# A fused attention and mixer kernel on one core: the first batch's steps in another order, and group 2's q and k loaded in pairs of heads over 128 rows

## The chip, the cores and the metric

The kernel runs on one core of a Trainium2 chip. Its engines run side by side, each through its own instructions in their order: TensorE (PE, matmuls), VectorE (DVE), ScalarE (ACT), GpSimd (POOL) and SyncE (SP, which only issues transfers). An engine waits where an instruction needs what another engine or a transfer has not yet delivered. Transfers between the memory outside (HBM) and the on-chip buffers of 128 partitions ("rows" below) are issued by SP, ACT or POOL and carried out by 16 DMA engines. The metric is the time of one execution in microseconds on the device; lower is better.

## The reference

For q, k, v of shape (8 batches, 12 heads, 448 tokens, 64) in float32:

```
q_n = q / sqrt(mean(q*q) + 1e-6) * g_q          # and k_n with g_k
x   = softmax(q_n k_n^T / 8) v                  # heads side by side: (8, 448, 768)
u   = x + mix(x)                                # over the tokens, (448x32) then (32x448)
out = u + max(u @ w_ch1, 0) @ w_ch2             # 768 -> 3072 -> 768
```

So each batch has attention with normalised q and k, a low-rank mix along the tokens, and a two-layer network, whose matmuls are most of the work.

## The kernel before

A batch's 12 heads are handled as three **groups** of four heads, a group as two **pairs** of two heads. The groups are numbered through: 0 to 2 are batch 0, 3 to 5 batch 1, and so on; pairs 0 and 1 belong to group 0, 2 and 3 to group 1, 4 and 5 to group 2.

For each group SP loads q, k and v as float32 (`load_qk` L93, `load_v` L106) into three rotating sets of buffers qf, kf, vf. A row holds two heads' share: row p of half `a` (64 rows) holds 7 tokens of head `c` = 0 and 7 of head `c` = 1. For most groups the heads of one half are two apart (0 and 2, or 1 and 3), so one transfer over 128 rows does it (L100). Group 2 (`BESIDE`) has neighbouring heads in a half: heads 0 and 1 of the group in the first 64 rows, 2 and 3 in the last. It is loaded by two transfers of 64 rows for q and two for k.

Then, per group: squares of q and k (steps `sq`, L136), their sums (`sm`, DVE, L166), the inverse roots by a logarithm and an exponential on ACT (`rt`, L942 to L953), scaling to bfloat16 (`sc`, L955), transposes on PE (`turn`, L363) and the copies out of them with q's gain (`tq` L371) or without (`tk` L380). v is cast by POOL (`val`, L204), and behind `val` of group g SP gets the loads of group g + 3. For group 0 the squares, sums, roots and scalings are cut in two parts (`sqp`, `smp`, `rt0`, `scp`).

Per pair: `S` (L418) computes four blocks of scores into one of two PSUM buffers, `E` (L433) takes their exponentials on ACT, `V` (L490) multiplies with v in two halves, and `N` (L507) divides by the row sums. Two sets of exponentials are kept, so a pair's first `E` waits for the `V` of the pair two before.

Batch 0 then is mixed (`mt`, `mtc`, `mix`, `mc`, L644 to L666) with matrices made from U and V (`prepu`, `prepv` on POOL), and its network starts (`u`, L706, the first four blocks; from L693 on the ordinary loop). `w` issues one part of the weights' load from POOL's queue (L295, L303); `b.n` issues n small matmuls that only keep PE busy (L242); `ms` clears buffers for the mix and, before the change, the zeros in the second key buffer (L345 to L348).

The order of all these steps for batch 0 is written out by hand in the text `FRONT` (L897); `name:engine` says which engine does a step (a ScalarE, v VectorE, p GpSimd). The steps are issued in that order, and every engine goes through its own share of them in that order. From batch 1 on a planner with fixed costs interleaves attention with the network; it doesn't see `FRONT`.

Of the kernel before, what the change touches and what calls it, by code (L numbers as in the profile page):

```python
# [27 lines left out]
def kernel(  # L28
# [13 lines left out]
    nc = tc.nc  # L42
    B, H, S, D = q.shape
# [5 lines left out]
    NT = S // 64  # L49
    NJ = S // P  # L50
    SM = NJ * P
    R = S - SM
# [32 lines left out]
    staged, ssqs, normed = {}, {}, {}  # L85
# [7 lines left out]
    def load_qk(gi, i, eng=None):  # L93
        b, h0, n = groups[gi]
        if gi == BESIDE:
            for a in range(2):
                nc.sync.dma_start(staged[gi][i][a * R:(a + 1) * R].rearrange("p (c j) d -> p c (j d)", c=2),
                                  (q, k)[i][b, h0 + 2 * a:h0 + 2 * a + 2].rearrange("c (p j) d -> p c (j d)", j=NT))
            return
        src = (q, k)[i][b, h0:h0 + n].rearrange("(c a) (p j) d -> (a p) c (j d)", a=2, j=NT)  # L100
        (eng or nc.sync).dma_start(staged[gi][i].rearrange("p (c j) d -> p c (j d)", c=2), src)
# [26 lines left out]
    def load(gi):  # L128
        stage_tiles(gi)
        for i in range(2):  # L130
            load_qk(gi, i)
        load_v(gi)
# [94 lines left out]
    for i in range(2):  # L227
        load_qk(0, i)
# [3 lines left out]
    for i in range(2):  # L232
        load_qk(1, i)
# [19 lines left out]
    def fill_values(i, eng):  # L253
        va, vl = va_bufs[i], vl_bufs[i]
        eng.memset(va[:, :, D:D1], 1.0)
        eng.memset(vl, 0.0)
        for e in range(2):
            eng.memset(vl[e * R:(e + 1) * R, :, e * D1 + D:(e + 1) * D1], 1.0)

    def fill_keys(i, eng):  # L260
        eng.memset(kT_bufs[i][D:P, :, SM:S], 0.0)
        eng.memset(kT_bufs[i][0:D, :, S:], 0.0)

    for i in range(2):
        fill_values(i, nc.vector)
    fill_keys(0, nc.vector)
    for e in range(2):
        nc.gpsimd.tensor_mul(gp[:, e * D:(e + 1) * D], grow[:, 0, :], grow[:, 1, :])

    gg = consts.tile([P, 2], FP32)  # L270
# [74 lines left out]
    def fill_mixer():  # L345
        nc.gpsimd.memset(Uz, 0.0)
        fill_values(2, nc.gpsimd)
        fill_keys(1, nc.gpsimd)  # L348


    at = {"pe": 0.0, "act": 0.0, "dve": 0.0}
# [429 lines left out]
    for i, (b, pr) in enumerate(pairs):  # L781
        if b == 0:
            continue
        gi, a = divmod(i, 2)
# [77 lines left out]
    for n, (c, f, a) in enumerate(att):  # L862
        gi = a[0] if f is Rest else a[2] if f is Spair else None
# [6 lines left out]
    for b in range(B):  # L870
# [24 lines left out]
    mlp.extend((3.9 * w, down_end, (B - 1, cols[-1], piece), B - 1) for piece, w in enumerate((1.0, 0.67, 0.34)))  # L895

    FRONT = """  # L897
        sqp.0.1:a sqp.0.0:p gr smp.0.1 sqp.1.1:a sqp.1.0:p smp.0.0 rt0.0.1 smp.1.1 gains:p smp.1.0 rt0.1.1 pg rt0.0.0 b.22
        scp.0.1:v scp.1.1:p rt0.1.0 scp.0.0:v sq.1.0:a scp.1.0:p gg turn.0.0 sm.1.0 ms tq.0.0:a turn.0.1 b.17 w tk.0.0 rt.1.0
        sq.1.1:a tq.0.1:v S.0.1 sc.1.0:v S.0.0 b.13 sq.2.0:p E.0.0 sm.1.1 turn.1.0 E.0.1 S.0.2 val.0 tk.0.1 E.0.2 tq.1.0:v b.5  # L900
        sm.2.0 S.0.3 b.8 E.0.3 S.1.0 rt.1.1 tq.1.1:v sq.2.1:p S.1.1 V.0.1 E.1.0 sc.1.1:v b.7 E.1.1 S.1.2 turn.1.1 sm.2.1 E.1.2
        S.1.3 V.0.0 tk.1.0 val.1 E.1.3 N.0.1 rt.2 tk.1.1 sc.2.0:p sc.2.1:v S.2.0 V.1.0 E.2.0 S.2.1 prepu N.1.0 E.2.1 S.2.2
        N.0.0 V.1.1 w E.2.2 turn.2.1 N.1.1 prepv S.2.3 b.4 tk.2.0 E.2.3 S.3.0 E.3.0 tk.2.1 S.3.1 w turn.2.0 V.2.0 E.3.1 tq.2.1:v
        S.3.2 N.2.0 mt.0 E.3.2 tq.2.0:v S.3.3 V.2.1 val.2 mtc.0 E.3.3 S.4.0 N.2.1 E.4.0 S.4.1 V.3.1 w V.3.0 E.4.1 N.3.1 S.4.2
        mix.1 N.3.0 E.4.2 S.4.3 sq.3.0:p mt.1 mc.1:v E.4.3 S.5.0 mtc.1 E.5.0 S.5.1 V.4.0 sq.3.1:p V.4.1 E.5.1 N.4.0 S.5.2 mix.0
        N.4.1 E.5.2 S.5.3 mix.2 mc.0:v mix.3 E.5.3 sm.3.0 u.0.0 mc.2:a u.1.0 mt.2 mc.3:a u.0.1 u.1.1 mtc.2 V.5.0 sm.3.1 u.2.0
        u.2.1 V.5.1 N.5.0 rt.3 u.3.0 u.3.1 N.5.1 u.0.3 u.1.3 u.2.3 u.3.3 mt.3 u.0.2 mix.4 mtc.3 u.1.2 mix.5 mc.4:a u.2.2 u.3.2
        mc.5:a u.0.4 u.1.4 u.2.4 u.3.4 u.0.5 u.1.5 u.2.5 u.3.5
    """
    engines = {"a": nc.scalar, "v": nc.vector, "p": pool, "": None}  # L910
    beside = uT.rearrange("p k c -> p (k c)")[:, :4 * NT * D].bitcast(FP32).rearrange("p (j d) -> p j d", d=D)
# [43 lines left out]
    def scale_by(gi, i, eng, lo=0, hi=NT):  # L955
# [8 lines left out]
        "smp": lambda i, p, eng: sums_part(i, *PARTS[p]),  # L964
        "rt0": lambda i, p, eng: (log_part(i, p), root_part(i, p)),
        "ms": lambda eng: fill_mixer(),
        "scp": lambda i, p, eng: scale_by(0, i, eng, *PARTS[p]),
        "gr": lambda eng: most_gain(),
# [82 lines left out]
    while ia < len(att) or im < len(mlp):  # L1051
# [10 lines left out]
        if take_att:  # L1062
            c, f, a = att[ia]
# [13 lines left out]
        else:  # L1077
# [6 lines left out]
            c, f, a, _ = mlp[im]  # L1084
# [35 lines left out]
```

## Time and profile before

| | |
|---|---|
| timed runs, us | 3262.81, 573.63, 570.91; median 573.63 |
| profiled execution, us | 570.46 (its span 568.7) |
| PE busy | 561.5 us, 99% |
| ACT, POOL, DVE busy | 308.5, 204.5, 189.4 us |
| the first matmul of L693 | at 39.46 us |
| loads of q and k, 448 KB each | 23 and 23, landing in 3.7 and 4.9 us in the median |
| group 2's q and k, 224 KB each | 2 and 2, landing in 7.8 and 6.4 us in the median |

The profile shows one execution. Busy time is an engine's instructions added up; its share of the span says which engine is full. Where an engine is idle, the row of the next instruction tells how long and what ended the wait. The chain of waits follows the work that ended last back to the start, at each step to what released it. Columns of the windows' rows are: the stretch, its length, then the busy time and instruction count of PE, weight loads, DVE, ACT and POOL, PE's granted clock, the busy share of the DMA engines and what they moved in GB/s. In rows of transfers stand the count, the size of one, and the median time from issue to landing.

### The profile page before, as it was taken

The page shows a single profiled execution, that of the slowest core. Times are in us where ns is not written, and L with a number is a line of the kernel's source. Part 1 is how long each engine was busy: PE and PEld are TensorE (multiplying, and loading weights), DVE is VectorE, ACT ScalarE, POOL GpSimd, SP SyncE. Part 2 cuts the span into 40 slices and gives each one's busy share as a digit, 9 for nine tenths or more (in the row PEclk, how much of TensorE's full clock was granted, in tenths as well). Part 3 has the DMA queues.
Part 4 walks back from the last instruction along what each step waited for, and adds up shares of the span by engine and source line. Part 5 has one row for each costly group of instructions (what it writes and reads, how often), then busy time and mean ns, then how long its engine had stood idle before and what let it go on. Part 6 is the DMA issues. An engine that isn't in the chain of part 4 may idle for free.

```text
span 568.7 us, 11567 instructions
## 1 busy us (share of the span) xinstructions
PE 561.5 (99%) x4756; PEld 321.9 (57%) x4756; DVE 189.4 (33%) x425; ACT 308.5 (54%) x518; POOL 204.5 (36%) x308
## 2 busy tenths in 40 slices
PE   8899999999999999999999999999999999999997
PEld 7665555555555555555556555565465555555555
DVE  6955564312443222521235231532034210410011
ACT  6967760888454776287553677367752544014300
POOL 6874784355332724343522532351531000000000
PEclk9999999999999999999999999999999999999999
DMA  9999999784247633595335735375215200320022
GB/s 241 223 242 240 247 228 179 159 225 114 62 91 171 170 98 63 90 233 144 74 96 107 203 90 125 67 204 128 36 33 86 56 23 0 77 56 0 1 57 56
DMA packets 104830, 68.20 MB, mean 120 GB/s; under 512 B 66633, under 2 KB 100937, under 8 KB 104777
## 3 DMA queue, kind: packets, MB, share of 16 engines
q1 hardware_dynamic: 95124, 57.83, 44.2%
q0 software_dynamic: 9408, 9.44, 10.0%
q8 instruction: 37, 0.61, 0.5%
q10 hardware_dynamic: 244, 0.20, 0.1%
q14 instruction: 17, 0.13, 0.1%
HBM read 52.20 MB, written 11.01 MB: 111 GB/s over the span
## 4 chain that ended last, share of the span: by engine, by line
PE 94%; ACT 4%; DMA 1%; DVE 0%; POOL 0%; issue 0%; POOLq 0%
PE po L740 38%; PE ph L693 37%; PE pv L541 4%; ACT E L435 3%; PE sc L464 2%; PE sl L455 2%; PE sl L476 2%; PE pr L568 1%; PE po L727 1%; PE pv L537 1%; PE sc L430 1%; PE sc L711 1%; PE sc L626 1%; PE pu L609 1%; DMA ob<-in_g_k_dram 1%; PE pt L368 1%
## 5 line engine op out<-in xcount | busy, mean ns | idle before, releaser
L693 PE MATMUL ph<-uT,w1b 128*128 128x448 bf16 x1128 | 223.9, 352 | 0.0
L740 PE MATMUL po<-w2b,hT 128*128 128x384 bf16 x1296 | 223.5, 326 | 0.0
L740 PEld LDWEIGHTS <-hT 128*128 128x128 bf16 x1296 | 122.8, 98 | 84.1 <-issue 7.0
L693 PEld LDWEIGHTS <-w1b 128*128 128x128 bf16 x1128 | 108.2, 98 | 97.6 <-issue 2.2
L700 ACT ACTIVATE hT<-ph 128x448 bf16<-128x448 f32 x187 | 99.7, 550 | 106.9 <-PE ph L693 106.5
L399 POOL TENSOR_SCALAR qT<-qT,gg 128x448 bf16<-128x448 bf16 x36 | 50.4, 1402 | 92.4 <-DMA qT<-qn 77.3
L457 ACT ACTIVATE E<-sl,gg 128x448 bf16<-128x448 f32 x72 | 41.6, 630 | 76.2 <-PE sl L455 75.3
L198 POOL TENSOR_TENSOR qn<-qf,rs 128x384 bf16<-128x384 f32 x36 | 29.9, 830 | 111.9 <-ACT rs L175 106.1
L468 ACT ACTIVATE E<-sc,gg 128x896 bf16<-128x896 f32 x72 | 68.9, 1019 | 0.0
L750 DVE TENSOR_TENSOR ob<-po,x 128x384 f32<-128x384 f32 x46 | 25.6, 557 | 103.7 <-PE po L740 103.0
L167 DVE TENSOR_REDUCE ssq<-sq 128x14 f32<-128x896 f32 x45 | 47.0, 1078 | 23.9 <-ACT sq L141 23.2
L545 DVE RECIPROCAL r<-pv 128x6 f32<-128x6 f32 x42 | 8.2, 195 | 125.4 <-PE pv L541 125.1
L435 ACT ACTIVATE E<-sc,gg 128x896 bf16<-128x896 f32 (+1 forms) x42 | 37.0, 951 | 1.1 <-PE sc L430 0.7
L541 PE MATMUL pv<-va,E 128*128 128x65 bf16 x756 | 35.4, 194 | 0.0
L541 PEld LDWEIGHTS <-E 128*128 128x128 bf16 x756 | 32.4, 98 | 3.2
L198 POOL TENSOR_TENSOR kp<-kf,rs 128x384 bf16<-128x384 f32 x36 | 29.8, 828 | 0.0
L537 PE MATMUL pv<-vl,E 128*128 128x130 bf16 x126 | 27.6, 219 | 0.0
L633 DVE TENSOR_TENSOR x<-sc,x 128x384 bf16<-128x384 f32 x42 | 20.8, 550 | 17.4 <-PE sc L626 17.4
L546 DVE TENSOR_TENSOR x<-pv,r 128x384 bf16<-128x384 f32 x42 | 23.4, 557 | 1.4
L174 ACT ACTIVATE rs<-ssq,eps 128x28 f32<-128x28 f32 x20 | 6.3, 315 | 32.1 <-DVE ssq L167 32.1
L477 ACT ACTIVATE E<-sl,gg 128x448 bf16<-128x448 f32 x36 | 23.3, 646 | 0.0
L206 POOL CAST va<-vf 128x768 bf16<-128x768 f32 x24 | 20.7, 862 | 0.2 <-DMA vf<-in_v_dram 0.2
(130 smaller groups left out, 426.4 us busy)
## 6 DMA issues: line engine op xcount, KB each, us to landing
qf<-in_q_dram SPq DMA_DIRECT2D x23, 448.0 KB, 3.7
kf<-in_k_dram SPq DMA_DIRECT2D x23, 448.0 KB, 4.9
vf<-in_v_dram SPq DMA_DIRECT2D x48, 192.0 KB, 5.5
out_dram<-ob SPq DMA_DIRECT2D x48, 192.0 KB, 2.7
w2b<-in_moe_w_ch_dram POOLq DMA_DIRECT2D x8, 576.0 KB, 15.3
w1b<-in_moe_w_ch_dram POOLq DMA_DIRECT2D x2, 1152.0 KB, 17.6
vf<-in_v_dram SPq DMA_DIRECT2D x48, 32.0 KB, 5.1
w1b<-in_moe_w_ch_dram POOLq DMA_DIRECT2D x1, 1536.0 KB, 28.5
```

Source lines behind the costliest of these rows:

```text
L167: nc.vector.tensor_reduce(ssqs[gi][:, i, :], sqs.pop((gi, i)), AX, ALU.add)
L198: nc.gpsimd.tensor_tensor(main.rearrange("p (t i) d -> p i t d", i=2), src[:, c, :2 * NJ].rearrange("p (i t) d -> p i t d", i=2), rs[:, c, ...
L399: nc.gpsimd.tensor_scalar(qT[:, a], qT[:, a], gg[:, 0:1], None, ALU.mult)
L435: nc.scalar.activation(es[(b, pr)][:, 2 * r:2 * r + n, :], sc[:, :n, :S], AF.Exp, scale=scal, bias=bias)
L457: nc.scalar.activation(E[:, 4 + i, :], ts[i], AF.Exp, scale=scal, bias=bias)
L468: nc.scalar.activation(E[:, 2 * r:2 * r + 2, :], tiles[r][:, :, :S], AF.Exp, scale=scal, bias=bias)
L537: nc.tensor.matmul(pv[:, i].rearrange("p e d -> p (e d)"), E[:, 2 * NJ, w:w + P], vl[:, lp, :], start=True, stop=False)
L541: nc.tensor.matmul(pv[:, i, e, :], E[:, 2 * j + e, w:w + P], va[:, (lp + 2 * e) * NJ + j, :], start=False, stop=(e == 1 and j == NJ - 1))
L693: nc.tensor.matmul(ph, w1b[:, dt, ht * P:(ht + 1) * P], uT[:, dt, off:off + S], start=(dt == 0), stop=(dt == KD - 1))
L700: nc.scalar.activation(hT[:, ht, off:off + S], ph, AF.Relu)
L740: nc.tensor.matmul(po, hT[:, ht, col:col + P], w2b[:, ht, half * HALF:(half + 1) * HALF], start=(ht == 0), stop=(ht == KH - 1))
L750: nc.vector.tensor_tensor(ob[:, h], po, urows(b, col, half), ALU.add)
```

## The change

Three edits.

1. Group 2's q and k are still loaded by two transfers each. Each now fills one of the two head slots (`c`) of all 128 rows, from two heads that are two apart, instead of both slots of 64 rows from two neighbouring heads. What lies where in the buffers afterwards is the same.
2. The zeros in the second key buffer are written by DVE at the start, with those of the first, instead of by POOL in `ms`.
3. `FRONT` has another order, other engines for some steps (sq.1.0 on POOL instead of ACT; sqp.1.0 and sqp.1.1 change places between ACT and POOL; scp.0.1 on POOL and scp.1.1 on DVE instead of the other way round; sc.1.0 on POOL instead of DVE) and other counts of the small matmuls (120 in all instead of 76).

```diff
         if gi == BESIDE:
-            for a in range(2):
-                nc.sync.dma_start(staged[gi][i][a * R:(a + 1) * R].rearrange("p (c j) d -> p c (j d)", c=2),
-                                  (q, k)[i][b, h0 + 2 * a:h0 + 2 * a + 2].rearrange("c (p j) d -> p c (j d)", j=NT))
+            for c in range(2):
+                nc.sync.dma_start(staged[gi][i][:, c * NT:(c + 1) * NT].rearrange("p j d -> p (j d)"),
+                                  (q, k)[i][b, h0 + c:h0 + c + 3:2].rearrange("a (p j) d -> a p (j d)", j=NT))
             return
...
-    fill_keys(0, nc.vector)
+    for i in range(2):
+        fill_keys(i, nc.vector)
...
         fill_values(2, nc.gpsimd)
-        fill_keys(1, nc.gpsimd)
...
     FRONT = """
-        sqp.0.1:a sqp.0.0:p gr smp.0.1 sqp.1.1:a sqp.1.0:p smp.0.0 rt0.0.1 smp.1.1 gains:p smp.1.0 rt0.1.1 pg rt0.0.0 b.22
-        scp.0.1:v scp.1.1:p rt0.1.0 scp.0.0:v sq.1.0:a scp.1.0:p gg turn.0.0 sm.1.0 ms tq.0.0:a turn.0.1 b.17 w tk.0.0 rt.1.0
-        sq.1.1:a tq.0.1:v S.0.1 sc.1.0:v S.0.0 b.13 sq.2.0:p E.0.0 sm.1.1 turn.1.0 E.0.1 S.0.2 val.0 tk.0.1 E.0.2 tq.1.0:v b.5
-        sm.2.0 S.0.3 b.8 E.0.3 S.1.0 rt.1.1 tq.1.1:v sq.2.1:p S.1.1 V.0.1 E.1.0 sc.1.1:v b.7 E.1.1 S.1.2 turn.1.1 sm.2.1 E.1.2
-        S.1.3 V.0.0 tk.1.0 val.1 E.1.3 N.0.1 rt.2 tk.1.1 sc.2.0:p sc.2.1:v S.2.0 V.1.0 E.2.0 S.2.1 prepu N.1.0 E.2.1 S.2.2
-        N.0.0 V.1.1 w E.2.2 turn.2.1 N.1.1 prepv S.2.3 b.4 tk.2.0 E.2.3 S.3.0 E.3.0 tk.2.1 S.3.1 w turn.2.0 V.2.0 E.3.1 tq.2.1:v
-        S.3.2 N.2.0 mt.0 E.3.2 tq.2.0:v S.3.3 V.2.1 val.2 mtc.0 E.3.3 S.4.0 N.2.1 E.4.0 S.4.1 V.3.1 w V.3.0 E.4.1 N.3.1 S.4.2
-        mix.1 N.3.0 E.4.2 S.4.3 sq.3.0:p mt.1 mc.1:v E.4.3 S.5.0 mtc.1 E.5.0 S.5.1 V.4.0 sq.3.1:p V.4.1 E.5.1 N.4.0 S.5.2 mix.0
-        N.4.1 E.5.2 S.5.3 mix.2 mc.0:v mix.3 E.5.3 sm.3.0 u.0.0 mc.2:a u.1.0 mt.2 mc.3:a u.0.1 u.1.1 mtc.2 V.5.0 sm.3.1 u.2.0
...
+        sqp.0.1:a sqp.0.0:p gr smp.0.1 gains:p sqp.1.0:a smp.0.0 sqp.1.1:p pg b.26 rt0.0.1 smp.1.0 rt0.0.0 scp.0.1:p smp.1.1
+        rt0.1.0 scp.0.0:v rt0.1.1 scp.1.0:p scp.1.1:v turn.0.0 sq.1.0:p gg turn.0.1 tq.0.0:a b.14 tk.0.0 sq.1.1:a S.0.0 w sm.1.0
+        S.0.1 b.17 E.0.0 sm.1.1 sq.2.0:p rt.1.0 S.0.2 b.18 E.0.1 tk.0.1 E.0.2 tq.0.1:v S.0.3 val.0 b.8 sm.2.0 rt.1.1 S.1.0 b.10
+        E.0.3 sc.1.1:v sc.1.0:p E.1.0 S.1.1 V.0.1 E.1.1 turn.1.1 S.1.2 sq.2.1:p tk.1.0 turn.1.0 E.1.2 S.1.3 V.0.0 tq.1.0:v E.1.3
+        tq.1.1:v S.2.0 N.0.1 E.2.0 val.1 S.2.1 b.11 sm.2.1 E.2.1 S.2.2 V.1.0 N.0.0 rt.2 tk.1.1 w V.1.1 E.2.2 S.2.3 sc.2.1:v b.9
+        w E.2.3 S.3.0 N.1.1 turn.2.1 E.3.0 sc.2.0:p N.1.0 S.3.1 V.2.1 E.3.1 tk.2.0 S.3.2 b.7 tk.2.1 E.3.2 ms turn.2.0 S.3.3
+        prepu V.2.0 tq.2.0:v E.3.3 tq.2.1:v S.4.0 prepv N.2.0 mt.0 E.4.0 S.4.1 mtc.0 V.3.0 val.2 E.4.1 S.4.2 N.3.0 V.3.1 E.4.2
+        N.2.1 w S.4.3 mix.0 N.3.1 E.4.3 mix.1 S.5.0 mc.0:v S.5.1 E.5.0 V.4.1 mc.1:v sq.3.0:p mt.1 N.4.1 E.5.1 S.5.2 V.4.0 mtc.1
+        E.5.2 sm.3.0 mix.3 sq.3.1:p mix.2 S.5.3 u.0.0 N.4.0 E.5.3 u.1.0 u.0.1 u.1.1 mc.2:a mt.2 sm.3.1 u.2.0 V.5.0 V.5.1 mtc.2
...
     """
```

More of the change, by code (lines that the diff above doesn't have):

```diff
@@ L906 @@
-        N.4.1 E.5.2 S.5.3 mix.2 mc.0:v mix.3 E.5.3 sm.3.0 u.0.0 mc.2:a u.1.0 mt.2 mc.3:a u.0.1 u.1.1 mtc.2 V.5.0 sm.3.1 u.2.0
-        u.2.1 V.5.1 N.5.0 rt.3 u.3.0 u.3.1 N.5.1 u.0.3 u.1.3 u.2.3 u.3.3 mt.3 u.0.2 mix.4 mtc.3 u.1.2 mix.5 mc.4:a u.2.2 u.3.2
-        mc.5:a u.0.4 u.1.4 u.2.4 u.3.4 u.0.5 u.1.5 u.2.5 u.3.5
+        sqp.0.1:a sqp.0.0:p gr smp.0.1 gains:p sqp.1.0:a smp.0.0 sqp.1.1:p pg b.26 rt0.0.1 smp.1.0 rt0.0.0 scp.0.1:p smp.1.1
+        rt0.1.0 scp.0.0:v rt0.1.1 scp.1.0:p scp.1.1:v turn.0.0 sq.1.0:p gg turn.0.1 tq.0.0:a b.14 tk.0.0 sq.1.1:a S.0.0 w sm.1.0
@@ new lines @@
+        prepu V.2.0 tq.2.0:v E.3.3 tq.2.1:v S.4.0 prepv N.2.0 mt.0 E.4.0 S.4.1 mtc.0 V.3.0 val.2 E.4.1 S.4.2 N.3.0 V.3.1 E.4.2
+        N.2.1 w S.4.3 mix.0 N.3.1 E.4.3 mix.1 S.5.0 mc.0:v S.5.1 E.5.0 V.4.1 mc.1:v sq.3.0:p mt.1 N.4.1 E.5.1 S.5.2 V.4.0 mtc.1
+        E.5.2 sm.3.0 mix.3 sq.3.1:p mix.2 S.5.3 u.0.0 N.4.0 E.5.3 u.1.0 u.0.1 u.1.1 mc.2:a mt.2 sm.3.1 u.2.0 V.5.0 V.5.1 mtc.2
+        rt.3 N.5.0 mix.4 mc.3:a u.2.1 N.5.1 u.3.0 mc.4:a u.3.1 u.0.3 u.1.3 mt.3 u.2.3 u.3.3 mtc.3 u.0.2 u.1.2 u.2.2 mix.5 u.3.2
@@ L909 @@
+        u.0.4 mc.5:a u.1.4 u.2.4 u.3.4 u.0.5 u.1.5 u.2.5 u.3.5
     """
```

## The prediction

> **What bounds the kernel now.** The page first: whether one engine fills the span, and at which clock.
>
> ```profile
> span 568.7 us, 11567 instructions
> PE 561.5 (99%) x4756; PEld 321.9 (57%) x4756; DVE 189.4 (33%) x425; ACT 308.5 (54%) x518; POOL 204.5 (36%) x308
> PEclk9999999999999999999999999999999999999999
> ```
>
> PE is busy for 99% of the span at full clock, and nothing in the change touches the multilayer part that fills it. So the question is when PE reaches that part, the first matmul of L693. The timeline of PE gives the place, the timeline of ACT what comes before it.
>
> ```profile
> 7.99 1.40 PE L245 MATMUL busy<-ident 128*128 128x128 bf16 x22
> ...
> 39.46 1.30 PE L693 MATMUL ph<-uT,w1b 128*128 128x448 bf16 x6
> ...
> 8.63 0.93 ACT L141 ACTIVATE sq<-qf 128x896 f32<-128x896 f32 x1
> ...
> 10.71 0.31 ACT L944 ACTIVATE rs<-ssq,eps 128x14 f32<-128x14 f32 x1
> ...
> 12.01 3.31 ACT L435 ACTIVATE E<-sc,gg 128x896 bf16<-128x896 f32 x4
> ...
> 18.85 0.33 ACT L944 ACTIVATE rs<-ssq,eps 128x28 f32<-128x28 f32 x1
> ...
> 19.43 13.55 ACT L435 ACTIVATE E<-sc,gg 128x896 bf16<-128x896 f32 x16
> 32.88 0.96 ACT L664 CAST uT<-ph 128x448 bf16<-128x448 f32 x2
> ```
>
> The front, the first batch's attention, takes 39.46 us. From 12.01 to 32.88 ACT goes from exponential to exponential almost without a gap; then 39.46 - 32.88 = 6.6 us of PE work end it. The chain of waits agrees: it runs over ACT there.
>
> ```profile
> 12.10 3.22 ACT E L435 x4
> ...
> 15.73 3.24 ACT E L435 x4
> ...
> 20.52 5.71 ACT E L435 x7
> ...
> 26.27 3.34 ACT E L435 x4
> ```
>
> The loads hide behind this only because they land early. The profiled execution took 570.46 us, 1.8 beyond its span; the three timed runs have a median of 573.63 with 570.91 as their lowest, so I work from 570.46. About 2%, here 11.4 us, is what a measurement of this kernel can tell from no change.
>
> **The change, the loads.** Group 2's q and k are now two transfers each of 224 KB as before, by 128 rows instead of 64. These rows show the present ones, their time to land, and the rates of all engines together (last column, GB/s; the share before it is of 16 engines).
>
> ```profile
> 2.78 1.42 SPq L97 DMA_DIRECT2D qf<-in_q_dram  x2
> ...
> 7.22 3.17 SPq L97 DMA_DIRECT2D kf<-in_k_dram  x2
> ...
> w1b<-in_moe_w_ch_dram POOLq DMA_DIRECT2D x1, 768.0 KB, 9.9
> ...
> qf<-in_q_dram SPq DMA_DIRECT2D x2, 224.0 KB, 7.8
> kf<-in_k_dram SPq DMA_DIRECT2D x2, 224.0 KB, 6.4
> ...
> ob<-in_moe_V_dram SPq DMA_DIRECT2D x1, 224.0 KB
> ...
> 2.00:3.00 1.00, 1.00 (x12) 1.00 (x11) 0.15 (x2) 0.01 (x1) 0.00 (x0) 1.00 0.91 224
> 3.00:4.00 1.00, 1.00 (x13) 1.00 (x10) 0.00 (x0) 0.00 (x0) 0.00 (x0) 1.00 1.00 353
> 4.00:5.00 1.00, 1.00 (x15) 1.00 (x14) 0.23 (x2) 0.52 (x1) 0.57 (x3) 1.00 1.11 378
> 5.00:6.00 1.00, 1.00 (x22) 1.00 (x20) 0.46 (x1) 0.45 (x2) 1.00 (x3) 1.00 0.96 344
> 6.00:7.00 1.00, 1.00 (x20) 0.91 (x17) 0.87 (x2) 0.45 (x3) 1.00 (x2) 1.00 1.03 364
> ...
> 13.00:14.00 1.00, 1.00 (x15) 0.65 (x12) 1.00 (x3) 1.00 (x2) 1.00 (x2) 1.00 1.10 237
> ```
>
> While 128-row loads run (3 to 7 us) all engines move 344 to 378 GB/s; later, with 64-row loads in flight, they are as busy and move 237. So 128 rows, dealt over all engines, would be the better form: 229 kB in 0.6 us.
>
> But the source of the new transfer has a pair of heads as its outermost dimension: the heads are two apart, so head and row don't merge into one dimension of 128, as they do in the loads of the other groups (L100), and the row isn't outermost, as it is in the present form (L98). If a transfer is dealt over the engines along its outermost dimension, the old form has 64 to deal and the new one 2: two engines carry it. One engine moves 378/16 = 23.6 GB/s, so 229 kB take 4.85 us on two engines, and the four transfers, if they share the same two, 19.4 us instead of the 2.4 that they would take on all. These are the two ends of the unknown price. No row settles it: moe_V's load, whose outermost dimension is 4 (L321), has a row without a time to land. I take two engines, because the code gives the dimension and the rows show nothing that could deal out a dimension of 2 to 16 engines.
>
> The Trainium skill, "DMA: Bandwidth & Descriptors", section "Why a DMA increments its semaphore by 16 and not by 1", states this: each access pattern's slowest dimension is looked at, and the largest count up to 16 that divides both sides is used, on the lowest-numbered engines. By it the new form runs on 2 engines, always the same two; no view of this profile shows the count.
>
> **The sum, along these two engines.** The four loads of groups 0 and 1 come first, 4 x 459 kB = 1.84 MB. The rows add up to 1.66 MB at 7.0 us, so they are through at 7.5. Group 2's q: two transfers, 9.7 us, to 17.2. Behind it in the queue stands each engine's share of group 0's v, 459/16 = 28.7 kB, at 237/16 = 14.8 GB/s 1.9 us; and the first weights, 768 KB issued by POOL, take their turns on the same engines, 49 kB each, 3.3 us: 22.4. Group 2's k: 9.7 us, 32.1; landed and seen, an estimate, at 33.
>
> What waits for it is in the rows of POOL and DVE (this square is group 2's k):
>
> ```profile
> 13.96 0.84 POOL L206 CAST va<-vf 128x768 bf16<-128x768 f32 x1
> ...
> 15.46 1.68 POOL L144 TENSOR_TENSOR sq<-kf 128x896 f32<-128x896 f32 x1
> 17.32 0.83 POOL L206 CAST va<-vf 128x768 bf16<-128x768 f32 x1 [0.18 <-DMA vf<-in_v_dram]
> ...
> 17.18 1.08 DVE L167 TENSOR_REDUCE ssq<-sq 128x14 f32<-128x896 f32 x1
> ...
> 22.55 0.90 POOL L295 DMA_DIRECT2D w1b<-in_moe_w_ch_dram  x1
> ```
>
> The square starts at 15.46 now and at 33 then. On POOL val.1, two weight issues and sc.2.0 are queued behind it (sc.2.0 from 33 + 1.7 + 1.5 + 1.8 = 38; it feeds the fifth pair's exponentials, due at about 41); on DVE N.0.0, tk.1.1 and sc.2.1 behind its sum; on ACT rt.2 waits for the sum, with E.2.2 and all later exponentials behind it. From 33: square 1.68, sum 1.08, rt.2 0.58 (18.85 to 19.43): 36.3. The row of sixteen exponentials lasts from 19.43 to 32.88, 13.45 us; in the new order two of them (E.2.0, E.2.1, 0.9 each) stand ahead of rt.2, so 13.45 - 1.8 = 11.65 are left: 48.0. Then the 6.6 us of the end: 54.6. L693 starts 54.6 - 39.5 = 15.1 us later, and since PE has no slack after it, the sum is 570.46 + 15.1 = **585.5 us**. V.0.1 slips too (val.0 waits for v, through at 22.4), but to about 24, well before 33.
>
> Loads behind these slip as well: v of groups 1 and 2, U and V are issued in order on SP behind them, and group 3's behind val.0. They land by about 40 to 50, when their users have slipped by the same 15. I take nothing for that and keep 3 us for the range.
>
> **The other edits.** The order by itself: sq.1.0 (0.93) leaves ACT for POOL and a part of the first squares comes back; rt.1.0 (0.31 and a second step) moves behind the first exponential. ACT gains at most 0.93 + 0.31, say 1 us, before its first exponential. ms moves on POOL from ahead of sq.2.0 to behind sc.2.0; the first weight issue stays ahead of sq.2.0, with sq.1.0 in front of it where ms was. The fillers grow from 76 to 120, 44 at 1.40/22 = 0.064, 2.8 us of PE; PE isn't the bound in the front, so they cost nothing as long as ACT is, and at most 2.8 if not. sm.3.0 now stands ahead of N.4.0 on DVE: if group 3's q lands late, N.4.0, mt.2 and the rest wait for it, up to 2 us by the row of group 2's k (6.4 to land). So the order alone lies between -1 and +3. Behind the late landing it is hidden; what it gives there is the two exponentials, already in the sum.
>
> ```profile
> 10.84 0.20 POOL L261 MEMSET kT<- 64x128 bf16 x1
> 11.10 0.20 POOL L262 MEMSET kT<- 64x128 bf16 x1
> ...
> 1.89 0.11 DVE L261 MEMSET kT<- 64x64 uint32 x1
> ...
> 4.77 0.21 DVE L276 TENSOR_REDUCE ob<-ob 1x1 f32<-1x64 f32 x1 [2.57 <-POOL ob L268]
> ```
>
> The zeros of the second key buffer leave POOL (two of 0.20) for DVE. DVE idles 2.57 us there, which hides them; without that cover they would cost about 0.2, two of 0.11.
>
> **Rivals.** *All engines.* The new loads are dealt over 16 engines. For it: 128 rows are what the fast loads have, 378 against 237 GB/s. Then k lands before 15.46 and the front stays ACT's: -1 for the order, **569.5**, no change or a little faster. It decides if k(2) lands before about 17. The Trainium skill, "DMA: Bandwidth & Descriptors", section "Rules for kernel authors", bids to replace two transfers to halves of the partitions by one of 128; by that rule alone this rival would hold, and the rates above agree with it for whole loads.
> *Two engines, but nothing queued behind.* If v and the weights pass the slow transfers instead of taking turns with them, 5.2 us go: k lands at 27.8, the end is 9.9 later, **580.5**.
> *Two engines and a longer trail.* Group 3 to 5's loads slip by more than PE does, or the two engines move less than 23.6 GB/s beside other traffic (14.8 as in the last rate row would give 7.8 us a transfer, 12 us more): 589.5 to 597, around **591**.
>
> **How the numbers follow.** Forecast 0.62, with a range of its own of 581.5 to 589 (k landing 4 us earlier or later); all engines 0.13; nothing queued 0.12; longer trail 0.13. The range 578 to 592 leaves out the first rival and 0.06 at the ends. Slower by over 2% (above 581.9): nearly all of the forecast and the long trail, 0.71; within 2%: 0.28; faster by over 2%: 0.01, since the front offers no 11 us that these edits could take.
>
> **What would show it.** In the changed kernel's DMA share a hollow between about 9 and 30 us, with few GB/s; POOL's square of group 2's kf (L144) waiting for its load until about 33, for some microseconds; ACT idle before rt.2; the first L693 at about 54. If kf is squared at 15 to 17 and no hollow shows, the step "two engines" is wrong. If the front is 15 us longer but the time isn't, PE has slack that I didn't see.

## The result, and the profile after

| | before | after |
|---|---|---|
| median of the timed runs, us | 571.83 (6 runs) | 590.94 (6 runs) |
| lowest and highest, us | 570.62 to 573.63, and a first run of 3262.81 | 589.51 to 593.5 |
| profiled execution, us | 570.46 | 593.22 |
| the first matmul of L693, us | 39.46 | 62.22 |
| profiled execution less that, us | 531.00 | 531.00 |

The change makes the kernel slower: the ratio is 1.0344, with an interval of 1.031 to 1.0378, or 19.1 us between the medians. The profile shows one execution, and it is one of the two longest of the six (593.2 and 593.5; the other four took 589.5 to 591.0). Its 22.8 us more lie entirely ahead of the first matmul of L693; the last row of the table says that nothing is gained or lost behind it.

The page of the changed kernel, the lines that answer to those of before and the DMA row of its 40 slices (14.8 us each):

```profile
span 591.4 us, 11655 instructions
PE 568.5 (96%) x4800; PEld 327.3 (55%) x4800; DVE 188.8 (32%) x426; ACT 308.9 (52%) x517; POOL 207.5 (35%) x308
PEclk9678999999999999999999999999999999999999
DMA  6469999978444763349452762268313410130022
```

PE has fallen from 99% to 96% of the span, and the second to fourth slices, up to 59 us, show a PE clock of 0.6 to 0.8, which the page of before doesn't. In the second and third the DMA engines are half idle although the kernel waits for loads. By stretches of 5 us (the last three columns are PE's granted clock, the busy share of the 16 DMA engines, and GB/s):

```profile
15.00:20.00 5.00, 0.66 (x9) 0.38 (x7) 0.00 (x0) 2.04 (x3) 0.00 (x0) 0.82 0.64 118
20.00:25.00 5.00, 0.00 (x0) 0.00 (x0) 2.08 (x2) 0.00 (x0) 2.90 (x4) 0.50 0.14 38
...
30.00:35.00 5.00, 1.40 (x24) 1.02 (x22) 0.00 (x0) 1.41 (x2) 1.35 (x1) 1.00 0.18 49
```

From 20 to 25 us the share is 0.14, and 0.14 of 16 is 2.2 engines (2.0 if measured against 1.12, the share from 45 to 50 us, when all are busy). In the trace a median of two packets are under way at a time in this stretch, and of 18 from 45 to 50 us. The two engines move 38 GB/s, 19 for each. That is a mean: loads of v and the weights take turns with q and k there. Where group 2's q or k moves alone, two engines move 50 to 52 GB/s, about 25 each:

```profile
8.00:9.00 1.00, 1.00 (x22) 1.00 (x20) 0.69 (x2) 0.35 (x2) 1.00 (x2) 1.00 0.13 52
...
24.00:25.00 1.00, 0.00 (x0) 0.00 (x0) 0.28 (x1) 0.00 (x0) 0.94 (x3) 0.50 0.13 50
```

Of the six such stretches of before, from 5 to 35 us, the following has the lowest share:

```profile
20.00:25.00 5.00, 4.60 (x67) 3.16 (x64) 4.76 (x18) 4.90 (x7) 4.88 (x8) 1.00 0.91 217
```

Who waits in this hollow is in the rows of POOL, DVE and ACT (start, duration; in brackets the idle time ahead and what ended it):

```profile
20.50 1.67 POOL L144 TENSOR_TENSOR uT<-qf 128x896 f32<-128x896 f32 x1 [8.80 <-DMA qf<-in_q_dram]
23.71 0.82 POOL L206 CAST va<-vf 128x768 bf16<-128x768 f32 x1 [1.55 <-DMA vf<-in_v_dram]
33.65 1.68 POOL L144 TENSOR_TENSOR sq<-kf 128x896 f32<-128x896 f32 x1 [6.75 <-DMA kf<-in_k_dram]
...
35.36 1.09 DVE L167 TENSOR_REDUCE ssq<-sq 128x14 f32<-128x896 f32 x1 [5.66 <-POOL sq L144]
...
36.48 0.32 ACT L944 ACTIVATE rs<-ssq,eps 128x28 f32<-128x28 f32 x1 [5.07 <-DVE ssq L167]
...
37.05 0.99 ACT L435 ACTIVATE E<-sc,gg 128x896 bf16<-128x896 f32 x1
38.49 0.63 ACT L435 ACTIVATE E<-sc,gg 128x448 bf16<-128x448 f32 x1 [0.45 <-PE sc L430]
39.94 1.01 ACT L435 ACTIVATE E<-sc,gg 128x896 bf16<-128x896 f32 x1 [0.82 <-PE sc L430]
...
51.16 0.63 ACT L435 ACTIVATE E<-sc,gg 128x448 bf16<-128x448 f32 x1 [0.29 <-PE sc L430]
```

Group 2's k is squared at 33.65 instead of 15.46; the sum, the root and every exponential from E.2.2 on stand behind it. The chain of waits ends the front with a second late load:

```profile
24.73 10.46 DMA vf<-in_v_dram
...
35.22 0.63 SPq L111
...
38.56 14.43 DMA kf<-in_k_dram
...
53.12 1.69 POOL sq L144
...
54.84 1.09 DVE ssq L167
55.92 0.21 DVE x L652
56.13 0.05 issue
56.18 0.56 PE ph L657
```

This is group 3's k. Its sum stands on DVE ahead of the copy (L652) that PE's mix needs. It was issued at 38.56, although val.0, behind which its load is placed, was over at 25.1. SP issues in order, and ahead of this load it had the rest of U, V and group 2's v: one load of U waited 3.4 us for group 2's k, and group 2's v (L111 at 35.22) for the v load issued at 24.73.

That it then took 14.4 us to land fits two weight loads of 1152 KB which POOL issued just ahead of it, from 36.67. The new order does the same with the old loads, and e8 and e9 below, which differ in the place of these two issues alone, show the price: group 3's k is squared at 36.69 in e8, after a wait for its load, and at 31.70 in e9, where the weights are issued behind it (and it is issued 1.3 us earlier), without a wait.

### The profile page after: what moved, and what is told of

Read it like the earlier page. It is cut to its first block, busy times and chain, and to the rows that moved or that the text cites. A ratio compares the mean times of both kernels' runs of the same rounds, so it can differ in the third digit from the quotient of the medians.

```text
span 591.4 us, 11655 instructions
## 1 busy us (share of the span) xinstructions
PE 568.5 (96%) x4800; PEld 327.3 (55%) x4800; DVE 188.8 (32%) x426; ACT 308.9 (52%) x517; POOL 207.5 (35%) x308
## 4 chain that ended last, share of the span: by engine, by line
PE 90%; DMA 5%; SPq 4%; ACT 0%; POOL 0%; DVE 0%; issue 0%; POOLq 0%
PE po L740 36%; PE ph L693 36%; PE pv L541 4%; DMA kf<-in_k_dram 2%; PE sc L464 2%; SPq L111 2%; PE sl L455 2%; DMA vf<-in_v_dram 2%; PE sl L476 2%; PE pr L568 1%; PE po L727 1%; PE pv L537 1%; SPq L97 1%; SPq L116 1%; PE sc L711 1%; PE sc L626 1%
## 5 line engine op out<-in xcount | busy, mean ns | idle before, releaser
L693 PE MATMUL ph<-uT,w1b 128*128 128x448 bf16 x1128 | 223.9, 352 | 0.0
L693 PEld LDWEIGHTS <-w1b 128*128 128x128 bf16 x1128 | 108.1, 98 | 97.7 <-issue 2.2
L167 DVE TENSOR_REDUCE ssq<-sq 128x14 f32<-128x896 f32 x45 | 47.0, 1079 | 32.9 <-ACT sq L141 23.2
```

What stands on the lines that cost most here:

```text
L167: nc.vector.tensor_reduce(ssqs[gi][:, i, :], sqs.pop((gi, i)), AX, ALU.add)
L693: nc.tensor.matmul(ph, w1b[:, dt, ht * P:(ht + 1) * P], uT[:, dt, off:off + S], start=(dt == 0), stop=(dt == KD - 1))
```

## The experiments

All of these compute the whole reference. Ratios are against the kernel before on the same chip, whose medians in the three groups of runs were 572.91, 571.86 and 571.35 us.

**e1, the order without the loads.** The changed kernel with the old loads:

```diff
-            for c in range(2):
-                nc.sync.dma_start(staged[gi][i][:, c * NT:(c + 1) * NT].rearrange("p j d -> p (j d)"),
-                                  (q, k)[i][b, h0 + c:h0 + c + 3:2].rearrange("a (p j) d -> a p (j d)", j=NT))
+            for a in range(2):
+                nc.sync.dma_start(staged[gi][i][a * R:(a + 1) * R].rearrange("p (c j) d -> p c (j d)", c=2),
+                                  (q, k)[i][b, h0 + 2 * a:h0 + 2 * a + 2].rearrange("c (p j) d -> p c (j d)", j=NT))
```

> The changed kernel with group 2's q and k loaded as before (64 rows at a time, the row outermost). Theory, two engines: the loss goes with the load, so 568 to 573 us, group 2's k squared at 15 to 18 us and L693 starting at 38 to 42. Rival, the order is what costs: about 588 to 592 us, L693 at 58 to 62 us, with the load landing early.

Measured: 577.45 us, ratio 1.0078 (1.0048 to 1.0109). The hollow and the long waits are gone, so the loads are the main part; but 4.5 us are left, more than the 3 that I had allowed the order. DVE's and PE's rows say where:

```profile
36.42 1.09 DVE L167 TENSOR_REDUCE ssq<-sq 128x14 f32<-128x896 f32 x1 [2.53 <-POOL sq L144]
37.42 0.17 DVE L513 RECIPROCAL r<-pv 128x4 f32<-128x4 f32 x1
37.63 0.42 DVE L514 TENSOR_TENSOR x<-pv,r 128x256 bf16<-128x256 f32 x1
39.82 1.09 DVE L167 TENSOR_REDUCE ssq<-sq 128x14 f32<-128x896 f32 x1 [1.76 <-POOL sq L144]
40.82 0.28 DVE L652 CAST x<-pu 128x128 bf16<-128x128 f32 x1
```

```profile
PE pu L648 <- DVE x L514: 2.1, 1, 2.1
PE ph L657 <- DVE x L652: 1.5, 1, 1.5
```

The sums of group 3's squares (L167) stand ahead of the division (L514) and of the copy (L652), wait 2.5 and 1.8 us for squares of data that has just landed, and PE waits behind them. The last exponential ends at 35.85 there, L693 starts at 47.04: an end of 11.2 us, with old loads.

**e2, the loads without the order.** The kernel before with the new form of the loads, the reverse of the diff above.

> The kernel before, with only the new load of group 2's q and k. Theory, two engines: k lands at about 33 us as in the changed kernel; all sixteen exponentials stand behind it here instead of fourteen, so at least as slow as the changed kernel, 589 to 595 us. Rival, the order is what costs: about 571 us.

Measured: 591.42 us, ratio 1.0323 (1.0283 to 1.0362), as much as the whole change. k is squared at 35.57:

```profile
35.57 1.68 POOL L144 TENSOR_TENSOR sq<-kf 128x896 f32<-128x896 f32 x1 [8.41 <-DMA kf<-in_k_dram]
```

The loads alone make the loss; that the order adds to it, or takes from it, doesn't show in the time. The rows do differ:

```profile
44.60 10.09 ACT L435 ACTIVATE E<-sc,gg 128x896 bf16<-128x896 f32 x12 [0.29 <-PE sc L430]
...
61.17 1.30 PE L693 MATMUL ph<-uT,w1b 128*128 128x448 bf16 x6
```

The last exponential ends at 54.69, 2.9 us later than in the changed kernel, and the end takes 6.5 us instead of 10.4. In the order of before the sums of group 3's squares start at 54.19 and 55.43 and hold nothing up, although its loads are as late (issued at 39.41 and 39.98).

**e3, the same bytes dealt by rows.** Each new transfer is cut into two of one head and 64 rows, so that the rows are the outermost dimension; the pieces that go to one row are as long as before.

```diff
-            for c in range(2):
-                nc.sync.dma_start(staged[gi][i][:, c * NT:(c + 1) * NT].rearrange("p j d -> p (j d)"),
-                                  (q, k)[i][b, h0 + c:h0 + c + 3:2].rearrange("a (p j) d -> a p (j d)", j=NT))
+            for a in range(2):
+                for c in range(2):
+                    nc.sync.dma_start(staged[gi][i][a * R:(a + 1) * R, c * NT:(c + 1) * NT].rearrange("p j d -> p (j d)"),
+                                      (q, k)[i][b, h0 + 2 * a + c].rearrange("(p j) d -> p (j d)", j=NT))
```

> The changed kernel with each of the four new transfers cut in two, one head and 64 rows each: the same head slots, the same 1792 bytes to a row, twice as many transfers, but the outermost dimension of the source is 64 and not 2. Theory, dealt along the outermost dimension: 568 to 574 us, k squared before 20 us. Rival, filling one head slot at a time in pairs of heads is what costs, whatever the engines: 588 to 592 us. A third, more transfers in the queue cost by themselves: between the two, about 575.

Measured: 579.21 us, ratio 1.0112 (1.0068 to 1.0156), about what e1 took: the order's cost, which I hadn't expected when I wrote 568 to 574, and little else. k is squared at 20.27, and its wait is no longer for the load:

```profile
20.27 1.68 POOL L145 TENSOR_TENSOR sq<-kf 128x896 f32<-128x896 f32 x1 [2.57 <-DVE x L515]
```

Bytes and the length of the pieces are those of the changed kernel, so these don't explain the loss. What differs is the outermost dimension, and that there are twice as many transfers of half the size. The number isn't it either: e1 has as many transfers as the changed kernel, with the 64 rows outermost, and its k doesn't wait.

**e4, the new form for q alone.** The kernel before with the new form of group 2's q; its k as before.

```diff
+            if i == 0:
+                for c in range(2):
+                    nc.sync.dma_start(staged[gi][i][:, c * NT:(c + 1) * NT].rearrange("p j d -> p (j d)"),
+                                      (q, k)[i][b, h0 + c:h0 + c + 3:2].rearrange("a (p j) d -> a p (j d)", j=NT))
+            else:
...
```

> The kernel before, with the new form for group 2's q alone and the old for its k. Theory, two engines in order: q through at 17.2 as worked out before, v at 22.4, then k's share on these engines, 28.7 kB at 14.8 GB/s, 1.9 us: k squared at about 25; then 3.35 to the root, 13.45 and 6.6: L693 at about 48.6, so about 580 us. Rival, only k's own transfers matter (what is queued behind q passes it): about 571 to 573 us.

Measured: 582.13 us, ratio 1.0164 (1.0126 to 1.0203); L693 starts at 51.66. Half of the slow loads cost half of the time, and what stands behind them on the queue waits with them: k, in its old form, is squared at 27.49, 2.5 us later than I expected.

**e5, small matmuls against the low clock.**

```diff
-... S.1.0 b.10
+... S.1.0 b.155
...
-        tq.1.1:v S.2.0 N.0.1 E.2.0 val.1 S.2.1 b.11 ...
+        tq.1.1:v S.2.0 N.0.1 E.2.0 val.1 S.2.1 b.100 ...
...
-... mc.2:a mt.2 ...
+... mc.2:a b.22 mt.2 ...
```

> The changed kernel with far more of the small matmuls that only keep PE busy: 155 instead of 10 ahead of the first pair's V.0.1, where PE waited 9.5 us for v, 100 instead of 11 behind S.2.1, where it waited 5.5 us, and 22 new ones ahead of mt.2. They give nothing to anyone. Theory 'clock': PE's waits lower its granted clock, and that makes the later scores and matmuls slow (0.2 to 0.8 us ahead of several exponentials, about 3 us up to 51.8, where my sum had 48.0). Then the granted clock in 20 to 60 us stays near 1.0, the last exponential ends 2 to 3 us earlier and the time is 587 to 589. Rival: the waits are only for loads, and group 3's k, landing at 53, sets the end whatever the clock: 590 to 592, the clock high all the same. If the small matmuls take longer than the waits they replace, 591 to 594.

Measured: 592.45 us, ratio 1.0361 (1.0317 to 1.0405). The granted clock was 1.00 from 10 to 30 and from 50 to 60 us, 0.89 and 0.94 in the two stretches of 10 us between, and the last exponential ended at 51.89 instead of 51.79. L693 came at 61.14, behind group 3's k, squared at 52.17. The theory's 587 to 589 is missed. The rival's 590 to 592 is nearer, but the clock wasn't high throughout as it said.

**e6, group 3's sums at the end.**

```diff
-        E.5.2 sm.3.0 mix.3 sq.3.1:p mix.2 S.5.3 u.0.0 N.4.0 E.5.3 u.1.0 u.0.1 u.1.1 mc.2:a mt.2 sm.3.1 u.2.0 V.5.0 V.5.1 mtc.2
-        rt.3 N.5.0 ...
+        E.5.2 mix.3 sq.3.1:p mix.2 S.5.3 u.0.0 N.4.0 E.5.3 u.1.0 u.0.1 u.1.1 mc.2:a mt.2 u.2.0 V.5.0 V.5.1 mtc.2
+        N.5.0 ...
...
-        u.0.4 mc.5:a u.1.4 u.2.4 u.3.4 u.0.5 u.1.5 u.2.5 u.3.5
+        u.0.4 mc.5:a u.1.4 u.2.4 u.3.4 u.0.5 u.1.5 u.2.5 u.3.5 sm.3.0 sm.3.1 rt.3
```

> The changed kernel with the sums of group 3's squares (sm.3.0, sm.3.1) and the root behind them (rt.3) moved from the middle of the front's end to its very end, behind the last network step of the first batch that the hand-written order holds. Nothing else is changed. Theory 'longer trail': group 3's q and k, issued behind the late val.0, land at up to 53 us, and N.4.0, mt.2 and the rest stand behind their sums on VectorE; without them the end takes about 7 to 8 us instead of 10.4, the first L693 starts at 58.5 to 59.5 and the time is 587 to 588.5. Rival 'clock alone': the end is longer because PE runs at half its clock there (2.06 us for five matmuls of L711): then nothing goes, L693 at 61.5 to 62.5, 590 to 592.

Measured: 590.67 us, ratio 1.0327 (1.0274 to 1.038). The mechanism shows: from the end of the last exponential (52.12 + 0.63) to L693 (58.67) it takes 5.9 us instead of 10.4. Of these 4.5 us the run keeps little. Its exponentials began 0.6 later (37.67), and behind L693 it takes 591.02 - 58.67 = 532.35 us instead of 531.00, because PE now waits for the scaling that the root was to feed:

```profile
PE pt L368 <- POOL qn L179: 1.0, 1, 1.0
```

The time itself, 590.67 beside 590.94, shows no gain. Group 3's sums were the mechanism of the long end in the profiled execution; that they cost the changed kernel several us in its median isn't shown.

**e7, v ahead of q and k.** Both loads of v are issued ahead of group 2's q and k.

```diff
-    load_qk(2, 0)
...
-    load_qk(2, 1)
+    load_qk(2, 0)
+    load_qk(2, 1)
```

> The changed kernel with the loads of groups 0's and 1's v issued ahead of group 2's q and k instead of between and behind them. Forecast by two engines with a queue: v(0) comes 9 to 12 us earlier, PE's wait of 9.5 us ahead of the first V goes, group 3's loads are issued earlier; q(2) lands 2 to 5 us later (22 to 25), and k(2) about where it did or 1 to 2 us later, 33.5 to 36, since the same bytes stand ahead of it on its two engines. The exponentials wait for k(2), so L693 moves with k(2): 592 to 594, or 588 to 590 if the earlier group 3 takes away the wait in the end. Rival: v's delay, not k's, is what costs: 576 to 583.

Measured: 591.88 us, ratio 1.0354 (1.0306 to 1.0402), and k squared at 36.46, both within 0.5 us of the forecast by the queue. v's delay isn't what costs. But q, squared at 26.46, came later than the 22 to 25 that I expected, and a step fell: PE's wait ahead of the first V grew to 13.4 us.

```profile
26.46 1.67 POOL L144 TENSOR_TENSOR uT<-qf 128x896 f32<-128x896 f32 x1 [14.67 <-DMA qf<-in_q_dram]
28.09 0.82 POOL L206 CAST va<-vf 128x768 bf16<-128x768 f32 x1
...
36.46 1.68 POOL L144 TENSOR_TENSOR sq<-kf 128x896 f32<-128x896 f32 x1 [5.18 <-DMA kf<-in_k_dram]
```

v is there, but its cast stands on POOL behind the square of q, which waits for q. I had followed the transfers' queue and forgotten POOL's. Group 3's loads come early enough here, and the end, from 53.86 to 59.78, takes 5.9 us with its sums in their place.

**e8, the order with the old loads and late sums.** e1 with the moves of e6.

> The new order with the old loads (as in e1_order_only, 577.45), and with sm.3.0, sm.3.1 and rt.3 at the very end. Theory: what the order alone costs (4.5 us) is N.4.0, mtc.2 and mt.3 standing on VectorE behind sums that wait for group 3's q and k, squared at 34.7 and 38.1 there; then L693 comes at 40 to 42 instead of 47.0 and the time is 570 to 573, no difference from the kernel before (572 to 573). Rival: the cost lies in the rest of the order (fillers, scalings on GpSimd, the late ms and prepu): 575.5 to 578. The theory's cousin, that the wait only moves to the next in the queue, gives 573.5 to 575.5.

Measured: 573.1 us, ratio 1.0017 (0.9994 to 1.004); L693 at 41.09, the end 5.9 us long. Against the kernel before on its chip (571.86) 1.2 of the 4.5 us are left, not clear of the noise: most of what the order cost lay in these three steps. The row of exponentials shows where more went, at a clock of 1.00:

```profile
21.14 4.25 ACT L435 ACTIVATE E<-sc,gg 128x896 bf16<-128x896 f32 x5
26.84 0.64 ACT L435 ACTIVATE E<-sc,gg 128x448 bf16<-128x448 f32 x1 [1.46 <-PE sc L430]
27.69 3.42 ACT L435 ACTIVATE E<-sc,gg 128x896 bf16<-128x896 f32 x4 [0.21 <-PE sc L430]
31.49 2.80 ACT L435 ACTIVATE E<-sc,gg 128x896 bf16<-128x896 f32 x3 [0.38 <-PE sc L430]
34.52 0.63 ACT L435 ACTIVATE E<-sc,gg 128x448 bf16<-128x448 f32 x1 [0.22 <-PE sc L430]
```

The fourteen exponentials behind rt.2 take 14.0 us here, where I had counted 11.65 from the order of before.

**e9 and e10, two mends of the order.** e9 is e8 with the two weight issues behind sc.2.0; e10 is e9 with group 3's sums and root ahead of u.0.5.

```diff
-... rt.2 tk.1.1 w V.1.1 E.2.2 S.2.3 sc.2.1:v b.9
-        w E.2.3 S.3.0 N.1.1 turn.2.1 E.3.0 sc.2.0:p N.1.0 ...
+... rt.2 tk.1.1 V.1.1 E.2.2 S.2.3 sc.2.1:v b.9
+        E.2.3 S.3.0 N.1.1 turn.2.1 E.3.0 sc.2.0:p w w N.1.0 ...
```

> The kernel of e8_order_late_sums with one move more: the two weight issues (w) that stand on GpSimd ahead of group 2's second scaling (sc.2.0) stand behind it. Theory: in the new order the exponentials lose about 2.3 us (gaps of 1.46, 0.21, 0.38 and 0.22) because TensorE waits 1.3 us in turn.2.0 for sc.2.0, which GpSimd starts at 24.31 behind 1.7 us of weight issues. Then that wait goes, the last exponential ends at 33.7 to 34.2 instead of 35.15, the first L693 starts at 39.6 to 40.2 instead of 41.09, and the time is 571 to 572.5. Rival: the gaps come from the order on TensorE itself (small matmuls and transposes ahead of the scores): they stay, 573 again. If the weights now land too late for the first network step, slower, 574 to 576.

```diff
-        u.0.4 mc.5:a u.1.4 u.2.4 u.3.4 u.0.5 u.1.5 u.2.5 u.3.5 sm.3.0 sm.3.1 rt.3
+        u.0.4 mc.5:a u.1.4 u.2.4 u.3.4 sm.3.0 sm.3.1 rt.3 u.0.5 u.1.5 u.2.5 u.3.5
```

> The kernel of e9_scale_first with the sums and the root of group 3 (sm.3.0, sm.3.1, rt.3) ahead of the sixth network step of the front (u.0.5) instead of behind the last. Theory: in e8 what follows the first L693 takes 532.4 us instead of the 531.0 of nearly all other kernels here, because the root stands on ScalarE behind the network's first two ReLUs (L714) and TensorE waits 1.0 us for GpSimd's scaling of group 3's q (L179). With the root ahead of them this wait goes, the rest takes 531.0 to 531.4 again and the time is 570 to 571.5, 1 us less than e9. Rival: the ReLUs come later by the root's 0.6 us, and L693 with them: no difference to e9.

Measured: 572.67 us, ratio 1.0024 (1.0011 to 1.0038), and 571.6 us, ratio 1.0014 (0.9993 to 1.0035). In e9 the gap of 1.46 us is gone, the last exponential ends at 34.29 and L693 starts at 40.24; the small gaps of 0.2 to 0.4 stay; the time, beside e8's 1.0017, shows no gain. In e10 PE's wait for the scaling is gone too, and from L693 on it takes 571.83 - 40.43 = 531.4 us. Neither beats the kernel before.

**e11, the clock held.** e6 with fillers that last until k is there.

```diff
-... S.1.0 b.10
+... S.1.0 b.155
...
-... val.1 S.2.1 b.11 ...
+... val.1 S.2.1 b.165 ...
```

> The kernel of e6_late_sums with 155 small matmuls instead of 10 ahead of V.0.1 and 165 instead of 11 behind S.2.1, which fill TensorE's waits of 9.3 and 5.2 us; they give nothing to anyone. The fillers of e5_fill ran out 2.5 us before k(2)'s sums came, and the clock was low again from 37.8 to 41. Theory 'clock': with the clock held until k(2) is there, the gaps of 0.45, 0.82, 0.34 and 0.47 us ahead of the first exponentials behind rt.2 shrink by 0.7 to 1.5 us, the granted clock is 0.95 or more from 10 to 60 us, and the time is 589 to 590 (e6: 590.67). Rival: the gaps stay at full clock, as those of e8 do, 590.5 to 591. Fillers that run on past the landing would cost up to 2 us: 592.

Measured: 590.56 us, ratio 1.0337 (1.0307 to 1.0367). Now the granted clock is 1.00 in every 10 us from 10 to 60. The fourteen exponentials take 13.0 us (from 40.07) instead of the 15.1 of e6, but they begin later, 1.18 us of it behind the fillers:

```profile
38.15 0.32 ACT L944 ACTIVATE rs<-ssq,eps 128x28 f32<-128x28 f32 x1 [6.04 <-DVE ssq L167]
...
40.07 1.01 ACT L435 ACTIVATE E<-sc,gg 128x896 bf16<-128x896 f32 x1 [1.18 <-PE sc L430]
41.35 0.63 ACT L435 ACTIVATE E<-sc,gg 128x448 bf16<-128x448 f32 x1 [0.27 <-PE sc L430]
```

So a low clock, with the work that piled up on PE, can stretch this row by up to 2.1 us; in the time nothing of it is left.

## Why the prediction was right, and where it wasn't

The forecast was 585.5 with a range of 578 to 592. The time is 590.94: inside that range, but 5.4 above the likeliest value, outside the forecast's own 581.5 to 589, and on the value of the rival "two engines and a longer trail" (around 591). The mechanism up to the landing of k was that of the forecast; two later terms were too small. That the rival's value was met is luck. The two engines did move less than 23.6 GB/s each beside other traffic (29 to 36 for both from 18 to 22 us), but k landed when it was forecast. Group 3's k did slip, by 23.7 us (squared at 53.12 instead of 29.43) where L693 slipped by 22.8. But with the same loads in the order of before (e2) it slips by 20.4 us, L693 by 21.7, and the end is no longer than it was: the cost comes with the new order.

**Two engines: right.** The share of 0.14 over 20 to 25 us is two engines of sixteen, and e3 shows that the same bytes with the rows outermost don't wait. This is the rule that the forecast quoted from the Trainium skill, "DMA: Bandwidth & Descriptors", section "Why a DMA increments its semaphore by 16 and not by 1". The count itself stands in no view; the share agrees with it. The rival "all engines" is refuted by e2.

**When k lands: right, the order of turns apart.** I had v through at 22.4 and k landed and seen at 33; v's cast starts at 23.71 and k's square at 33.65. The 23.6 GB/s of one engine holds where nothing else is under way: the two move 50 to 52 when q or k is alone, and from v's cast to k's square are 9.9 us, for a forecast of 9.7. But q, forecast for 17.2, was squared at 20.50, because the weights, which I had put behind q, took their turns while it still moved: from 18 to 20 us POOL's queue moved 26 packets and SP's 24. What they took beside q they no longer took behind it, so k came when it was forecast. "Nothing queued behind" is refuted: v's cast waits until 23.71, and in e4 k, in its old form, lands late behind the new q.

**From the landing to the next exponential: right.** 36.3 forecast, 37.05 measured, the 0.65 of the landing included.

**The exponentials: 11.65 forecast, 14.7 measured (37.05 to 51.79), 3.1 too few.** I took their length from the order of before, where they follow without a gap. The new order's own gaps are in e8: 14.0 us at full clock, of which e9 gave back the one for sc.2.0. In the changed kernel they come with a PE at half clock that has to catch up behind V.1.1; in e11, at full clock, 13.0 us remain. In e2, in the order of before, the sixteen take 15.4 us (39.29 to 54.69) instead of 13.45, with a clock of 0.50 to 0.52 from 35 to 45 us. The step that failed is "so 13.45 - 1.8 = 11.65 are left", which asked only what ACT itself has to do.

**The end: 6.6 forecast, 10.4 measured, 3.8 too few.** The prediction put what follows of group 3's late loads at nothing and kept 3 us in the range. Their k landed at 53, later than the 40 to 50 it named, and their sums stood in front of the end. The late loads alone don't make it long: e2 has them too, and its end takes 6.5 us, as forecast; e1, with the old loads in the new order, has 11.2. So the term that was missed belongs to the new order, which puts the sums ahead of N.4.0 and mtc.2 and two weight loads ahead of group 3's. The prediction saw the first ("up to 2 us") and called it hidden behind the late landing; it isn't hidden, since it stands behind the exponentials. With the sums moved to its very end it takes 5.9 us both with the new loads (e6) and the old (e8), and 5.9 again in e7, where these loads come earlier.

With the 0.75 up to the first exponential the three terms make 7.6 us, the difference between the measured 62.22 and the forecast 54.6. In the median 5.4 us of it remain; I have no profile of one of the shorter executions and can't say which term is smaller there.

**The order alone: wrong.** I bounded it at -1 to +3; e1 measured 4.5. The row that I used for sm.3.0 ahead of N.4.0 (up to 2 us) was that of one wait; the second sum, ahead of mtc.2, waits again. That the order is hidden behind the loads is right for the time alone (e2 and the whole change take the same), and by luck: the 2.9 us that the new order gives up to the last exponential are taken back by the 3.9 us of its longer end.

**No slack in PE: right.** What follows the first L693 took 531.0 us in the kernels before and after and in e1, e2 and e4, 531.1 in e7, 531.3 in e5. Where it is longer (532.2 to 532.4 in e6, e8, e9 and e11, 531.4 in e10) group 3's root had been moved. In e3 it is 532.2, for a reason that I haven't found.

## What to carry to other kernels

Before making a transfer wider, write down its dimensions after merging and look at the outermost one: a wide tile loaded through an outermost dimension of 2 had two engines here and cost 19 us, and everything behind it on the queue paid too. The sign of it in a profile is a DMA share near 0.14 while engines wait for a load. When a late landing moves a stage, don't move the old stage's length as a block: ask which other load and which in-order queue (here DVE's sums, POOL's square ahead of v's cast, SP's own issues) now arrives late inside it.

## What the runs showed of the hardware that I had not expected

The granted clock of TensorE fell to 0.50 while PE waited for these loads (20 to 25 us, no instruction in that stretch), and its matmuls took 1.6 times as long afterwards: the scores of L430 0.56 us at the low clock, 0.35 in e11.

```profile
37.89 0.56 PE L430 MATMUL sc<-qT,kT 128*128 128x448 bf16 x1
```

```profile
40.96 0.35 PE L430 MATMUL sc<-qT,kT 128*128 128x448 bf16 x1
```

The Trainium skill, "TensorE: Matmul & The Clock Gate", section "Part 1: The HAM clock gate (the "warmup" mystery)", states this: half the clock after an idle window of about 3.4 us, full again after a busy one. The trace agrees in the main, with 0.50 in a wait of 9.5 us and 1.00 in e11, where small matmuls fill the waits but for 2.8 us. By estimates from rows of 1 us (a clock of 0.60 from 18 to 19, 0.78 from 28 to 29 and 0.63 from 35 to 36 us) it fell 2.5 us after PE's last matmul (15.66) the first time and 3.7 us (31.53) the second, and was full again 3.3 us after PE went on (25.18). In the profile of before the clock is full in every slice, so I left it out of the sum; but a front with new waits has a new clock.

SP's own issues slowed as well. The two transfers of group 2's k took SP 6.22 us to issue instead of the 3.17 of before, and those of group 0's v, behind the new q, 5.58 us instead of 1.41:

```profile
4.42 5.58 SPq L111 DMA_DIRECT2D vf<-in_v_dram  x2
...
13.63 6.22 SPq L97 DMA_DIRECT2D kf<-in_k_dram  x2
```

So the slow loads held back not only what was queued behind them but also what SP still had to issue. What in SP's issue waits, no run here shows.
